# A weight shift done in place, two softmax norms on another engine, and a saturating add in the first block of tokens

## The chip, the cores and the metric

The kernel runs on one core of one Trainium2 chip. The core has five engines that run side by side: TensorE (PE; its weight loads are shown as PEld), VectorE (DVE), ScalarE (ACT), GpSimd (POOL) and SyncE (SP, which here only issues transfers). The metric is the device time of one execution in microseconds, lower is better.

## The reference

Three stages, each feeding the next. The attention is masked in two ways: the first half of the heads sees a window of 32 keys, the second half every fourth key of the last 128.

```
# attention: q, k, v are (4, 8, 576, 64)
scores = scale * q @ k.T
scores = where(mask, scores, -1e9); attn = softmax(scores)
x = (attn @ v) as (2304 tokens, 512)
# first feed-forward: w_in (512, 2048), w_out (2048, 512)
h = x @ w_in
x = (h * cos(h)) @ w_out
# second feed-forward: w1, w2, w3 (512, 768), w_out (768, 512)
h = maximum(maximum(x @ w1, x @ w2), x @ w3)
out = h @ w_out
```

The weights arrive as 64-bit floats, as the reference's setup draws them, and the kernel turns them into 32-bit floats on the chip.

## The kernel before, in words

**Precision.** A matrix product is made of three passes of a fast 32-bit format. Each operand is split into a high part and a low part (`g_hi` and `g_lo`, `w_hi` and `w_lo`), and the products high*high, low*high and high*low are summed in PSUM.

**Stages.** The tokens of the first feed-forward are cut into five blocks (four of 512, one of 256). First comes the attention of the 12 units that block 0 needs (about 7 to 48 us). Then `ff1` runs 16 steps per block, one per slice of 128 hidden columns. A step `s` makes `h` for its slice (12 matrix products, line 358), and the output sums for slice `s - 3` (12 products, line 401). `h` has two PSUM banks that alternate (`h_bank`, `bank_98` and `bank_99` in the rows; step 2 alone has `bank_97`), so step `s + 2` can start only when VectorE has read the bank of step `s` for the last time (line 390). In between stand the attention units of the next block: scores (lines 268 to 275), exponentials (217), norm (303 to 307), transposes (315), output (326 to 345).

**Steps 0 to 15 do one thing more.** They turn the 32 weight tiles of the first feed-forward from 64 into 32 bits: `w_exponent` on ScalarE (line 183) rescales the high words in place, `w_bits` on VectorE (lines 188 and 191) joins the words into `wx`, and `w_halves` splits the result on ScalarE (line 143, `w<-wx`) and GpSimd (line 208). `wx` has two buffers, and a buffer is free again when GpSimd is done with it. In block 1 and later, `raw_bits` (lines 437 and 440) does the same for the weights of the second feed-forward on tiles of half the size, and there the shift already writes in place.

**The cosine.** `ff1_reduce` brings the argument into the range of the sine table. The table `ENGINES` says which engine does what, with one entry for each of four phases: the attention of block 0, block 0 of `ff1` (16 steps), the blocks after that, and the last block. In phase 1 the entry `turns` is `"A"`: ScalarE makes the number of turns `kk` as a rounded integer (line 372), and VectorE makes `r = hv - 2 pi kk` (line 378) and clips it (line 381). Then ScalarE takes the sine (line 217), VectorE multiplies by `hv` (line 390) and the product is split (lines 143 and 392).

**Norms.** The entry `norm` of phase 0 is `"VPP"`: of the 12 units of the first attention, units 0, 3, 6 and 9 have their norm (line 307) on VectorE and the others on GpSimd.

**Order.** The code writes one program, and a scheduler with a cost model of its own sets the order of the instructions on each engine. So an edit in one place moves instructions around it too. Every engine runs its own instructions in that order, and one that waits holds up all that stand behind it.

Of the kernel before, what the change touches and what calls it, by code (L numbers as in the profile page):

```python
# [2 lines left out]

# [4 lines left out]

F32 = mybir.dt.float32
# [2 lines left out]
I32 = mybir.dt.int32  # L12
I64 = mybir.dt.int64
AF = mybir.ActivationFunctionType
ALU = mybir.AluOpType
# [34 lines left out]
ARG_HI = 1.5707960  # L50
ARG_LO = -4.7123880
# [5 lines left out]
ENGINES = {  # L57
    "w_hi": ("A", "A", "A", "V"),
    "w_lo": ("P", "P", "P", "PV"),
    "norm": ("VPP", "V", "V", "V"),  # L60
    "pt": ("A", "A", "V", "V"),
    "ring": ("A", "A", "V", "V"),
    "turns": ("V", "A", "V", "V"),
# [34 lines left out]
def body(  # L98
# [11 lines left out]
    nc = tc.nc  # L110
# [20 lines left out]
    def engine(work):  # L131
        names = ENGINES[work][phase[0]]
        turn[work] = turn.get(work, 0) + 1
        return names[(turn[work] - 1) % len(names)]
# [50 lines left out]
    def bits(x, w):  # L185
        pair = w.bitcast(I32).rearrange("p (n two) -> p n two", two=2)
        low, high = pair[:, :, 0], pair[:, :, 1]
        nc.vector.tensor_scalar(
            out=x, in0=high, scalar1=3, scalar2=None, op0=ALU.logical_shift_left
        )  # L190
        nc.vector.scalar_tensor_tensor(
            out=x, in0=low, scalar=29, in1=x, op0=ALU.logical_shift_right, op1=ALU.bitwise_or
        )

    def w_exponent(key):
# [2 lines left out]
    def w_bits(key):  # L198
        x = wx.tile([128, 512], I32, tag="x", name="wx")
        bits(x, words[key])  # L200
        words[key] = x.bitcast(F32)
# [13 lines left out]
    def activation(*args, **kw):  # L215
        with tc.issue_after(last_table[-1]) if last_table else nullcontext():
            last_table.append(nc.scalar.activation(*args, **kw).ins)  # L217
# [150 lines left out]
    def ff1_reduce(s, hv):  # L368

        kk = tmp.tile([128, TB], F32, tag="r", name="kk")[:, : hv.shape[-1]]  # L370
        if engine("turns") == "A":
            nc.scalar.activation(kk.bitcast(I32), hv, AF.Copy, scale=INV2PI, bias=0.25)
        else:
            nc.vector.tensor_scalar(  # L374
                out=kk.bitcast(I32), in0=hv, scalar1=INV2PI, scalar2=0.25, op0=ALU.mult, op1=ALU.add
            )
        r = tmp.tile([128, TB], F32, tag="r", name="r")[:, : hv.shape[-1]]
        nc.vector.scalar_tensor_tensor(  # L378
            out=r, in0=kk.bitcast(I32), scalar=-2.0 * math.pi, in1=hv, op0=ALU.mult, op1=ALU.add
        )  # L380
        nc.vector.tensor_scalar(  # L381
            out=r, in0=r, scalar1=ARG_HI, scalar2=ARG_LO, op0=ALU.min, op1=ALU.max
        )
        activation(r, r, AF.Sin, bias=hpi)
        g[s] = (hv, r)

# [447 lines left out]
    for s in range(NS + LAG):  # L834
# [17 lines left out]
        if s < NS:  # L852

            hv = (bank[3] if s == 2 else h_bank[(s + (s > 2)) % 2])[:, : BLOCKS[t]]
# [5 lines left out]
        for j, (kind, x, c) in enumerate(chunks):  # L860
            if kind == "h":
                hc(x, c)
                if x == NC - 1:
                    hvs[s] = hv
                    ff1_reduce(s, hv)
            else:
                t0, f0 = divmod(s - LAG, NF1)
                acc_chunk(STARTS[t0], f0 == 0, f0 == NF1 - 1, halves[("out", f0)], g[s - LAG], x)
            while done < len(pieces) and done * len(chunks) < (j + 1) * len(pieces):
                do, u = pieces[done]  # L870
                do(u)
                done += 1
            if j == 1:
                if s >= 1 and s - 1 < NS:
                    ff1_g(s - 1)
            if s < NF1:
                weights(STEP_WEIGHTS[s].count(j), WSLOTS)
            if j == 1:
                raw_exponent(s - NF1)
            if j == 5:  # L880
                raw_bits(s - NF1)
# [94 lines left out]
```

## Time and profile before

| what | value |
|---|---|
| median of 3 runs | 832.45 us (832.4 to 833.21) |
| the profiled execution | 830.6 us, its span 828.8 us |
| busy in the span: PE, DVE, ACT, POOL | 795.8, 571.3, 430.9, 134.1 us |
| mean granted TensorE clock | 0.983 of 2.4 GHz |

The span is the time from the first to the last instruction that the profiler saw on the core. What lies around it, 1.8 us here, is part of the time of the execution. A busy TensorE need not be one at its peak, since the ends of matrix products are modelled.

### The profile page before, as it was taken

What the parts mean: (1) busy time and instruction counts of PE and PEld (TensorE: products, weight loads), DVE (VectorE), ACT (ScalarE), POOL (GpSimd) and SP (SyncE); (2) the same over time, 40 slices, a digit from 0 to 9 for tenths busy, and PEclk for the clock granted to TensorE, in tenths of its full rate; (3) what the DMA queues carried; (4) which work ended last, traced back from release to release, by engine and by line L of the source; (5) the groups of instructions that cost most, each with busy time, mean ns of one, the idle gap of its engine ahead of it and who ended that gap; (6) DMA issues with size and microseconds to landing.
All of it is one profiled execution on the core that took longest, in us unless ns stands there. A gap on an engine that the chain in (4) does not pass through costs nothing.

```text
span 828.8 us, 12969 instructions
## 1 busy us (share of the span) xinstructions
PE 795.8 (96%) x4484; PEld 679.8 (82%) x4484; DVE 571.3 (69%) x1499; ACT 430.9 (52%) x1004; POOL 134.1 (16%) x120
## 2 busy tenths in 40 slices
PE   7867999999999999999999999999999999999998
PEld 6645767677777877777878889998899999999997
DVE  5888899768887788888686676878873355615540
ACT  5977988657765287774442234365452324422321
POOL 1354445410000000000000002225520000000000
PEclk8968999999999999999999999999999999999999
DMA  9982111234334343333020015636783778537812
GB/s 349 418 335 79 36 49 51 73 124 136 108 99 127 119 150 96 110 127 123 28 70 10 1 50 182 237 143 264 268 303 107 210 260 253 172 121 258 249 34 76
DMA packets 52625, 124.43 MB, mean 150 GB/s; under 512 B 5840, under 2 KB 18768, under 8 KB 52560
## 3 DMA queue, kind: packets, MB, share of 16 engines
q1 hardware_dynamic: 52560, 123.61, 43.8%
q8 instruction: 35, 0.57, 0.3%
q14 instruction: 30, 0.25, 0.1%
HBM read 91.34 MB, written 32.24 MB: 149 GB/s over the span
## 4 chain that ended last, share of the span: by engine, by line
PE 67%; DVE 12%; DMA 11%; ACT 4%; issue 3%; POOL 2%; SPq 1%; ACTq 0%; POOLq 0%; DVEq 0%
PE bank L586 20%; PE bank L401 16%; PE bank L358 15%; PE bank L651 9%; PE bank L268 3%; DMA w<-in_w_in 3%; DMA w<-in_w_out 2%; DMA wh<-in_w 2%; PE bank L326 2%; PE bank L315 1%; DVE ws L510 1%; DMA wd<-wh 1%; ACT e L217 1%; DMA raw<-wd 1%; DVE r L378 1%
## 5 line engine op out<-in xcount | busy, mean ns | idle before, releaser
L358 PE MATMUL bank<-ring,w 128*128 128x512 f32 (+1 forms) x960 | 235.3, 383 | 7.4 <-DVE r L390 6.3
L401 PE MATMUL bank<-gt,w 128*128 128x512 f32 (+1 forms) x960 | 225.3, 376 | 0.0
L586 PE MATMUL bank<-ring,wa 128*128 128x384 f32 x1134 | 200.5, 335 | 3.7 <-DVE mx L616 2.6
L586 PEld LDWEIGHTS bank<-ring,wa 128*128 128x128 f32 x1134 | 196.4, 188 | 6.2 <-DVE mx L616 3.7
L358 PEld LDWEIGHTS bank<-ring,w 128*128 128x128 f32 x960 | 166.4, 192 | 42.5 <-DVE r L390 8.2
L401 PEld LDWEIGHTS bank<-gt,w 128*128 128x128 f32 x960 | 164.9, 189 | 33.4 <-issue 0.3
L217 ACT ACTIVATE r<-r,hpi 128x512 f32<-128x512 f32 (+1 forms) x80 | 54.5, 681 | 93.9 <-DVE r L381 93.3
L217 ACT ACT_TABLE_LOAD x62 | 79.5, 1283 | 32.5 <-DVE r L381 25.6
L217 ACT ACTIVATE e<-e,m 96x128 f32<-96x128 f32 x192 | 74.8, 391 | 6.2 <-DVE m L275 5.6
L651 PE MATMUL bank<-g,w 128*128 128x384 f32 x432 | 76.3, 334 | 0.0
L651 PEld LDWEIGHTS bank<-g,w 128*128 128x128 f32 x432 | 75.0, 188 | 0.0
L390 DVE TENSOR_TENSOR r<-bank,r 128x512 f32<-128x512 f32 (+1 forms) x80 | 50.5, 632 | 21.5 <-ACT r L217 21.5
L139 POOL TENSOR_SCALAR gt<-r 128x512 fp32r<-128x512 f32 x24 | 16.1, 673 | 296.8 <-PE bank L401 229.2
L275 DVE CUSTOM_DVE_ANT_0 e<-bank,cs 96x128 f32<-96x128 f32 x192 | 45.7, 282 | 20.7 <-PE bank L271 10.1
L374 DVE TENSOR_SCALAR kk<-bank 128x512 int32<-128x512 f32 (+1 forms) x64 | 39.7, 621 | 19.2 <-PE bank L358 16.7
L208 POOL TENSOR_TENSOR w<-wx,w 128x512 fp32r<-128x512 f32 x32 | 44.7, 1410 | 48.8 <-ACT w L143 47.5
L378 DVE SCALAR_TENSOR_TENSOR r<-kk,bank 128x512 f32<-128x512 int32 (+1 forms) x80 | 50.3, 629 | 1.6 <-DMA x1d<-o 0.2
L392 DVE TENSOR_TENSOR gt<-r,gt 128x512 fp32r<-128x512 f32 (+1 forms) x65 | 40.4, 621 | 14.1 <-POOL gt L139 10.6
L268 PEld LDWEIGHTS bank<-qkv 64*96 64x96 f32 x288 | 26.0, 163 | 26.9 <-issue 8.7
L602 ACT COPY s<-bank 128x384 f32<-128x384 f32 x54 | 25.8, 478 | 37.9 <-PE bank L586 36.5
L268 PE MATMUL bank<-qkv 64*96 64x128 f32 x288 | 38.5, 295 | 6.9 <-DVE m L275 3.7
L620 DVE TENSOR_TENSOR s<-s,bank 128x384 f32<-128x384 f32 x36 | 19.8, 551 | 34.3 <-PE bank L586 34.2
(65 smaller groups left out, 848.7 us busy)
## 6 DMA issues: line engine op xcount, KB each, us to landing
wa<-opd SPq DMA_DIRECT2D x54, 512.0 KB, 4.6
opd<-wa SPq DMA_DIRECT2D x27, 512.0 KB, 2.8
qkv<-in_qkv SPq DMA_DIRECT2D x36, 336.0 KB, 2.9
wh<-in_w SPq DMA_DIRECT2D x36, 256.0 KB, 2.7
w<-in_w_in SPq DMA_DIRECT2D x16, 512.0 KB, 9.3
w<-in_w_out SPq DMA_DIRECT2D x16, 512.0 KB, 9.8
qkv<-in_qkv SPq DMA_DIRECT2D x12, 432.0 KB, 9.1
wd<-wh SPq DMA_DIRECT2D x36, 128.0 KB, 1.8
```

The source lines that it names most:

```text
L208: tensor("w_lo").tensor_tensor(out=w[:, 1, :], in0=x, in1=w[:, 0, :].bitcast(F32), op=ALU.subtract)
L217: last_table.append(nc.scalar.activation(*args, **kw).ins)
L268: nc.tensor.matmul(sv, q[rows], k[rows], start=True, stop=True)
L275: nc.vector.tensor_tensor_reduce(out=e[:, 2 * j + h, :], in0=places_of[j, h], in1=mask[:, kind, :], scale=-1.0 / math.sqrt(D), scalar=3e38 ...
L358: nc.tensor.matmul(hv, w[:, a, 128 * c : 128 * c + 128], ring[c][:, x, c0 : c0 + n_tok], start=n == 0 and j == 0, stop=n == NC - 1 and j == 2,
L374: nc.vector.tensor_scalar(out=kk.bitcast(I32), in0=hv, scalar1=INV2PI, scalar2=0.25, op0=ALU.mult, op1=ALU.add)
L378: nc.vector.scalar_tensor_tensor(out=r, in0=kk.bitcast(I32), scalar=-2.0 * math.pi, in1=hv, op0=ALU.mult, op1=ALU.add)
L390: nc.vector.tensor_tensor(out=r, in0=hv, in1=r, op=ALU.mult)
L392: tensor("g_lo").tensor_tensor(out=gt[:, 1, :], in0=r, in1=gt[:, 0, :].bitcast(F32), op=ALU.subtract)
L401: nc.tensor.matmul(a_dm, w[:, a, 128 * dm : 128 * dm + 128], gt[:, x, :], start=first and n == 0, stop=last and n == 2,)
L586: nc.tensor.matmul(out, ops[q][a][:, x, 128 * c : 128 * c + 128], b_op(b, c)[:, y], start=first and c == 0 and n == 0, stop=c == 1 and n == 2,
L651: nc.tensor.matmul(a, wo[2 * f + r][:, x, 128 * dm : 128 * dm + 128], g2[f, r, n][:, y], start=f == 0 and r == 0 and k == 0, stop=f == NF2 ...
```

## The change

Three edits. In `w_bits` the shift of the high words (line 188) writes into the tile of the 64-bit weights itself and not into `wx`; the joining instruction (line 191) reads both words there and is the first to write `wx`. In `ENGINES` the norm's entry for phase 0 names all 12 units one by one: units 10 and 11 go from GpSimd to VectorE, the others stay. In `ff1_reduce`, where `turns` is `"A"` (block 0 alone), ScalarE also multiplies `kk` by `-2 pi`, and one VectorE instruction, `TENSOR_ADD_SAT`, adds `hv` and clips; the two VectorE instructions of lines 378 and 381 stay for the other blocks.

```
-    "norm": ("VPP", "V", "V", "V"),
+    "norm": ("VPPVPPVPPVVV", "V", "V", "V"),
...
         nc.vector.tensor_scalar(
-            out=x, in0=high, scalar1=3, scalar2=None, op0=ALU.logical_shift_left
+            out=high, in0=high, scalar1=3, scalar2=None, op0=ALU.logical_shift_left
         )
         nc.vector.scalar_tensor_tensor(
-            out=x, in0=low, scalar=29, in1=x, op0=ALU.logical_shift_right, op1=ALU.bitwise_or
+            out=x, in0=low, scalar=29, in1=high, op0=ALU.logical_shift_right, op1=ALU.bitwise_or
         )
...
-        if engine("turns") == "A":
+        e = engine("turns")
+        if e == "A":
             nc.scalar.activation(kk.bitcast(I32), hv, AF.Copy, scale=INV2PI, bias=0.25)
...
-        nc.vector.scalar_tensor_tensor(
-            out=r, in0=kk.bitcast(I32), scalar=-2.0 * math.pi, in1=hv, op0=ALU.mult, op1=ALU.add
-        )
-        nc.vector.tensor_scalar(
-            out=r, in0=r, scalar1=ARG_HI, scalar2=ARG_LO, op0=ALU.min, op1=ALU.max
-        )
+        if e == "A":
+
+            nc.scalar.activation(r, kk.bitcast(I32), AF.Copy, scale=-2.0 * math.pi)
+            nc.vector._custom_dve(dve_ops.TENSOR_ADD_SAT, out=r, in0=hv, in1=r, s0=ARG_HI, s1=ARG_LO)
+        else:
+            nc.vector.scalar_tensor_tensor(
+                out=r, in0=kk.bitcast(I32), scalar=-2.0 * math.pi, in1=hv, op0=ALU.mult, op1=ALU.add
+            )
+            nc.vector.tensor_scalar(
+                out=r, in0=r, scalar1=ARG_HI, scalar2=ARG_LO, op0=ALU.min, op1=ALU.max
+            )
```

What the scheduler makes of it, at two places. The first is ScalarE from the first `kk` of block 0 (bank_98 holds step 0, bank_99 step 1, bank_97 step 2) to the first sines. Before:

```order
L372 ACTIVATE kk<-bank_98 128x512
L143 CAST w<-wx 128x512
L372 ACTIVATE kk<-bank_99 128x512
L183 ACTIVATE w_284<-w_284 128x512
L143 CAST w<-wx 128x512
L217 ACT_TABLE_LOAD
L217 ACTIVATE r<-r,hpi 128x512 x2
L183 ACTIVATE w_286<-w_286 128x512
L372 ACTIVATE kk<-bank_97 128x512
```

The same stretch of the changed kernel, where line 373 is the old 372 and line 381 is the new multiplication:

```order
L373 ACTIVATE kk<-bank_98 128x512
L143 CAST w<-wx 128x512
L381 ACTIVATE r<-kk 128x512
L373 ACTIVATE kk<-bank_99 128x512
L143 CAST w<-wx 128x512
L217 ACT_TABLE_LOAD
L217 ACTIVATE r<-r,hpi 128x512
L381 ACTIVATE r<-kk 128x512
L183 ACTIVATE w_286<-w_286 128x512
L373 ACTIVATE kk<-bank_97 128x512
L217 ACTIVATE r<-r,hpi 128x512
```

The multiplication stands one weight cast behind its `kk`, and the second sine has moved behind the second multiplication, one exponent instruction and the third `kk`.

The second place is VectorE from the first high part of a product (`gt<-r`, step 0) to the first scores of block 1 (line 275). Before:

```order
L143 CAST gt<-r 128x512
L378 SCALAR_TENSOR_TENSOR r<-kk,bank_97 128x512
L188 TENSOR_SCALAR wx<-w_286 128x512
L381 TENSOR_SCALAR r<-r 128x512
L191 SCALAR_TENSOR_TENSOR wx<-w_286,wx 128x512
L188 TENSOR_SCALAR wx<-w_288 128x512
L191 SCALAR_TENSOR_TENSOR wx<-w_288,wx 128x512
L188 TENSOR_SCALAR wx<-w_290 128x512
L275 ISA e,m<-bank_100,cs 96x128
```

The same stretch of the changed kernel, where line 382 is the saturating add and line 396 the old 390:

```order
L143 CAST gt<-r 128x512
L188 TENSOR_SCALAR w_286<-w_286 128x512
L191 SCALAR_TENSOR_TENSOR wx<-w_286 128x512
L396 TENSOR_TENSOR r<-bank_99,r 128x512
L382 ISA r<-bank_97,r 128x512
L188 TENSOR_SCALAR w_288<-w_288 128x512
L191 SCALAR_TENSOR_TENSOR wx<-w_288 128x512
L275 ISA e,m<-bank_100,cs 96x128
```

One shift and one instruction of the reduction have gone from in front of the scores, and the last product of step 1 (bank_99), which stood ahead of the cast before, has come in.

## Rows read from the trace of the kernel before

**Rows 1.** The page's first part: busy time, share of the span, instructions.

```profile
PE 795.8 (96%) x4484; PEld 679.8 (82%) x4484; DVE 571.3 (69%) x1499; ACT 430.9 (52%) x1004; POOL 134.1 (16%) x120
```

**Rows 2.** Windows by stage: window, PE, PEld, DVE, ACT, POOL busy, granted clock, DMA.

```profile
48.00:70.00 22.00, 13.87 (x48) 10.05 (x48) 19.69 (x34) 16.43 (x31) 12.26 (x9) 0.72 0.76 287
70.00:160.00 90.00, 85.95 (x477) 63.01 (x476) 77.34 (x208) 75.13 (x192) 40.61 (x29) 0.98 0.15 45
400.00:500.00 100.00, 100.00 (x479) 82.07 (x478) 69.18 (x138) 34.35 (x64) 6.34 (x9) 1.00 0.11 35
```

**Rows 3.** Timeline, end of the first attention: start, duration, instruction, idle before.

```profile
41.48 1.37 POOL L307 TENSOR_TENSOR e<-e,z 96x512 f32<-96x512 f32 x1 [0.71 <-DVE z L304]
41.91 0.96 DVE L303 TENSOR_SCALAR z<-z 96x4 f32<-96x4 f32 x1
42.90 0.65 PE L315 MATMUL bank<-cs,e 96*128 96x96 f32 x4 [1.31 <-POOL e L307]
...
44.34 0.74 PE L315 MATMUL bank<-cs,e 96*128 96x96 f32 x3 [0.79 <-POOL e L307]
45.55 1.48 DVE L188 TENSOR_SCALAR wx<-w 128x512 int32<-128x512 int32 x1 [2.23 <-POOL w L208]
```

**Rows 4.** Timeline, from the first `kk` to step 3 on TensorE.

```profile
52.32 0.60 ACT L372 ACTIVATE kk<-bank 128x512 int32<-128x512 f32 x1 [1.95 <-PE bank L358]
...
53.50 1.30 POOL L208 TENSOR_TENSOR w<-wx,w 128x512 fp32r<-128x512 f32 x1 [2.03 <-ACT w L143]
53.55 1.79 DVE L191 SCALAR_TENSOR_TENSOR wx<-w,wx 128x512 int32<-128x512 int32 x1
...
56.07 1.28 ACT L217 ACT_TABLE_LOAD   x1
...
57.37 1.40 ACT L217 ACTIVATE r<-r,hpi 128x512 f32<-128x512 f32 x2
...
58.53 1.27 DVE L390 TENSOR_TENSOR r<-bank,r 128x512 f32<-128x512 f32 x2
...
59.27 4.21 PE L358 MATMUL bank<-ring,w 128*128 128x512 f32 x9 [4.31 <-DVE r L390]
```

**Rows 5.** Timeline, in front of the first scores of block 1.

```profile
61.72 1.51 DVE L381 TENSOR_SCALAR r<-r 128x512 f32<-128x512 f32 x1
...
63.15 1.75 DVE L191 SCALAR_TENSOR_TENSOR wx<-w,wx 128x512 int32<-128x512 int32 x1
...
67.13 1.47 DVE L188 TENSOR_SCALAR wx<-w 128x512 int32<-128x512 int32 x1 [1.17 <-POOL w L208]
...
69.29 0.88 PE L268 MATMUL bank<-qkv 64*96 64x128 f32 x8 [3.75 <-DVE m L275]
```

**Rows 6.** Groups on DVE, 70 to 160 us: busy, mean ns, idle before.

```profile
L275 DVE CUSTOM_DVE_ANT_0 e<-bank,cs 96x128 f32<-96x128 f32 x44 | 10.6, 279 | 4.4 <-PE bank L268 2.7 <-PE bank L315 1.3 <-ACT kk L372 0.3
...
L378 DVE SCALAR_TENSOR_TENSOR r<-kk,bank 128x512 f32<-128x512 int32 x11 | 7.4, 674 | 0.0
L381 DVE TENSOR_SCALAR r<-r 128x512 f32<-128x512 f32 x11 | 6.4, 586 | 0.0
```

**Rows 7.** Groups on ACT, 70 to 160 us.

```profile
L143 ACT CAST w<-wx 128x512 fp32r<-128x512 f32 x19 | 11.5, 616 | 3.4 <-DVE wx L191 3.4
L183 ACT ACTIVATE w<-w 128x512 f32<-128x512 f32 x15 | 9.7, 676 | 0.0
```

**Rows 8.** Chain that ended last, share by line, 70 to 160 us.

```profile
by line: PE bank L401 15.8%; PE bank L358 13.9%; issue 13.8%; PE bank L268 7.0%; POOL w L208 7.0%; ACT e L217 4.9%; DVE e L307 4.8%; DVE wx L188 4.0%; DVE wx L191 4.0%; DVE r L381 3.4%; DVE e L275 3.2%; PE bank L326 2.8%; DVE ring L345 2.6%
```

**Rows 9.** Lines by themselves: least, median and most ns; first and last start.

```profile
L188 DVE TENSOR_SCALAR wx<-w x32: 393/417/1502, 11.5 to 155.3; 128x512 int32<-128x512 int32 x32
L191 DVE SCALAR_TENSOR_TENSOR wx<-w,wx x32: 673/688/1793, 12.8 to 156.3; 128x512 int32<-128x512 int32 x32
L437 DVE TENSOR_SCALAR wh<-wh x48: 258/285/299, 161.5 to 398.1; 128x256 int32<-128x256 int32 x48
L378 DVE SCALAR_TENSOR_TENSOR r<-kk,bank x80: 410/679/689, 52.9 to 543.2; 128x512 f32<-128x512 int32 x64, 128x256 f32<-128x256 int32 x16
```

More of the change, by code (lines that the diff above doesn't have):

```diff
@@ L5 @@
 import concourse.tile as tile
-from concourse import mybir
+from concourse import dve_ops, mybir
 from concourse._compat import with_exitstack
```

## The prediction

> **What bounds the kernel now.** I read the busy times of the page first: TensorE is busy for 96% of the span, so a gain has to come from where it is not, or from where it is slow [rows 1]. The windows by stage say where that is. Late in the kernel it has no idle time (400 to 500 us: 100.00 of 100). From 48 to 70 us it is busy for 13.87 of 22 us at a granted clock of 0.72, and from 70 to 160 us for 85.95 of 90 while VectorE has 77.34 and ScalarE 75.13 [rows 2]. That is block 0 of `ff1`, the only place where `w_bits` and the changed branch of the cosine run.
>
> Then I read the timeline at TensorE's two long waits there. They add up to 4.31 + 3.75 = 8.06 of the 8.13 idle us between 48 and 70 [rows 2, 4, 5]. The first ends when VectorE has made the product of step 0 (line 390), the second when it has read the first scores of block 1 (line 275). What the reader is to see in the rows ahead of them are VectorE instructions that last far too long. The join of line 191 takes 0.688 us in the median, but 1.79 where it starts 0.05 us after a GpSimd split; it ends at 55.34, the split at 54.80, so it did nearly all its work after the split [rows 4, 9]. The shift of line 188 (median 0.417, most 1.502), line 381 (1.51) and even the tiny line 303 (0.96 us for 4 columns, until GpSimd's norm ended) behave alike [rows 3, 5, 9]. Line 378, with one input in PSUM, is never held: most 0.689 against a median of 0.679 [rows 9]. So VectorE is the engine that is late here, and part of its lateness is being held behind GpSimd.
>
> **The shift in place.** Same instruction, other destination. Line 437 is that form on half the size: 0.285 us for 256 elements, where line 188 takes 0.417 for 512 [rows 9]. The difference, 0.132 us for 256 elements, is 0.52 ns each; line 191's 0.688 for 512 is at least twice that. So the form in place runs at the fast rate too: one that didn't would take more than 0.285 for 256. So the price is 0, and the shift can still be held by GpSimd. What goes is its wait for a free `wx`, 2.23 and 1.17 us in two places [rows 3, 5]. It doesn't vanish: the join of line 191 is now the one that waits for the buffer. Only the shift's own 0.417 moves in front of the wait. I count 0.4 us, once, on the path; bounds 0 and 2.2 (the first wait wholly gone).
>
> **The two norms.** Unit 10's norm ran on GpSimd from 41.48 for 1.37 us, and TensorE went on at 42.90; unit 11's let it go on at 44.34, after 1.31 and 0.79 us of idling [rows 3]. On VectorE a norm reads 512 elements from two SBUF inputs, as line 191 does: 0.688 us if not held [rows 9]. It would be ready near 42.6, 0.3 earlier. But GpSimd is then free to take the next weight split, and this holds VectorE at unit 11's norm for up to 1.3 us [rows 4]: 43.5 at best, 44.6 at worst. I take 0, bounds -0.3 and +0.9.
>
> **The cosine, first wait.** From the start of the first `kk` (52.32) to TensorE's next product (59.27) it is 6.95 us now [rows 4]. In the new order ScalarE runs `kk`, a weight cast, the multiplication, the second `kk`, another cast, the table load and the first sine. Durations: 0.60 for `kk`; 0.616 for a cast; the multiplication is new, and its nearest rows are two ScalarE instructions over 512 elements in SBUF, 0.616 and 0.676, so 0.65 [rows 4, 7]; 1.28 for the table; half of 1.40 for a sine and half of 1.27 for the product [rows 4]. Sum: 0.60 + 0.62 + 0.65 + 0.60 + 0.62 + 1.28 + 0.70 + 0.64 = 5.71. The saturating add lies under the second `kk`, the cast and the table load, with 2.50 us of cover; without it it would cost its 0.69. Gain 6.95 - 5.71 = 1.2. Each of the two casts waits for a join, and a held join is 1.1 late [rows 4]: bounds -1.0 and, if ScalarE's instructions overlap, +2.0.
>
> The add itself is not in this trace. A custom VectorE instruction of 128 elements takes 0.279 us, a plain one of 512 with the same kind of inputs 0.674 [rows 6]. With 0.674 as the lower bound and four times 0.279, 1.12, as the upper, I take 0.685: the small custom instruction shows no extra start cost. One input in PSUM, like line 378, so I expect it never to be held.
>
> **The cosine, second wait.** From the cast in `gt` to the scores VectorE now has, unheld, 0.68 + 3 x 0.417 + 0.42 + 2 x 0.688 = 3.73 us of work (lines 378, 188, 381, 191), and rows 5 show 1.09 + 1.06 + 1.05 us of holding and 1.17 of waiting on top, 4.37 together. The new order has 2 x 0.417 + 2 x 0.688 + 0.68 + 0.685 = 3.58 of work, and four instructions there can be held at some 1.1 each. None held gives all of TensorE's 3.75; all four nothing. With two held: 4.37 - 2.2 + 0.15 = 2.3. Behind the scores stand the exponentials and with them all attention of block 1, so this is not given back at once.
>
> **The cosine, steps after 70 us.** VectorE loses 11 x (0.674 + 0.586) and gets 11 x 0.685: 6.3 us less of 77.34. ScalarE gets 11 x 0.65 = 7.2 more on 75.13, so 82.3 us of work [rows 2, 6]. Not all of the relief counts. The chain of waits has line 381 on it for 3.4% of these 90 us, 3.1 us [rows 8]; that is my term. Bounds: 0, and 90 - 82.3 = 7.7, where ScalarE would never idle.
>
> **Sum.** 0 + 0.4 + 1.2 + 2.3 + 3.1 = 7.0 us. The profiled execution took 830.6 (span 828.8 and 1.8 around it), so 823.6 for its like; the median of before is 1.85 above it: 825.4. All upper bounds together (0.9 + 2.2 + 2.0 + 3.75 + 7.7) would be 816, all lower ones (-0.3 - 1.0) 833.8. About 0.2%, 1.7 us, is what a measurement tells from no change.
>
> **Rivals.** *ScalarE fills up.* With 82.3 us of work in a stretch that is to shrink to 87, an engine that runs in order and also carries exponentials and table loads has little slack. Then the term of 3.1 goes and one held cast takes 1.1 from the first wait: 832.45 - 2.8 = 829.6. For it: its busy share would be 95%. Against: VectorE was at 86% and still on the path, so the load alone does not decide.
>
> *Slower: the sine comes later in every step.* From `kk` to sine it is 0.60 + 0.674 + 0.586 = 1.86 us now, and 0.60 + 0.62 + 0.65 + 0.69 = 2.56 with one cast in between, 0.7 later; 1.8 later where that cast waits for a held join. The place is the cast between lines 373 and 381 in the changed order. Over the 11 steps this is 7.7 to 20 us if the two `h` banks make TensorE wait for it each time. It decides from about ten steps at 0.7 or four at 1.8, which cancels the 7.0. Halfway, at 1.05 a step, it gives 11.6 - 7.0 = 4.6 slower: 837. Against: TensorE idles only 4.05 us in the 90 [rows 2], so the banks leave room. The Trainium skill (ScalarE: Activation LUTs, Rules for kernel authors) advises VectorE and not ScalarE for `mul` and `add`, and by that rule the move is a loss; the rows agree that the multiplication was free on VectorE, inside line 378, and show that VectorE is the late one.
>
> *Hidden anyway.* The holding by GpSimd finds another VectorE instruction each time, and the two waits stay: 832.
>
> *More.* Less idling may also keep the granted clock up (0.72 in this stretch [rows 2]), and most of the 7.7 comes in: 818.
>
> **How the numbers follow.** Forecast (821 to 829) 0.55; ScalarE fills up 0.13; slower 0.11; hidden 0.10; more 0.11. Faster 0.79, same 0.10, slower 0.11. The range 818 to 832.5 leaves out the slower case and about half of the largest.
>
> **What would show it.** The add at 0.67 to 0.70 us, none above 0.75; the multiplication at 0.62 to 0.68; line 188 still at 0.417 in the median, with no wait for `wx`, and waits in front of line 191 instead; TensorE's two waits near 3.1 and 1.5 us; VectorE's share of the stretch down by some 6 us, ScalarE's up by 7. Wrong if the add is held behind GpSimd, if the sines wait for the multiplication, or if the time after block 0 moves by itself.

## The result, and the profile after

The changed kernel takes 827.0 us in the median of 5 runs (823.42 to 828.71), beside 833.21 (832.4 to 835.62) for the kernel before on the same chip. The ratio is 0.9911, with a 95% interval of 0.9894 to 0.9927: faster by 0.9%, some 7.4 us. All ratios below are of 4 to 12 runs of a kernel against the kernel before, timed beside it, with the 95% interval in brackets; gains in us go by the ratio. The profiled execution took 827.17 us, its span 825.4. In the changed kernel line 372 has become 373, 390 is 396, 401 is 407 and 411 is 417; line 381 is the new multiplication and 382 the saturating add.

The page's first part, and the windows by stage (columns as in [rows 2]):

```profile
PE 793.4 (96%) x4484; PEld 678.6 (82%) x4484; DVE 567.1 (69%) x1485; ACT 439.2 (53%) x1020; POOL 132.9 (16%) x118
```

```profile
48.00:70.00 22.00, 17.16 (x70) 11.79 (x68) 17.81 (x47) 19.05 (x43) 13.12 (x9) 0.77 0.74 287
70.00:160.00 90.00, 87.52 (x489) 64.80 (x489) 73.98 (x179) 79.64 (x197) 41.71 (x30) 1.00 0.16 44
```

Against [rows 2], TensorE is busy 3.3 us more in the 22 us of the ramp and 1.6 us more in the 90 behind it. VectorE has lost 3.4 us there and ScalarE has gained 4.5.

The timeline of the changed kernel: the last norms, then from the first `kk` to step 3, then in front of the scores.

```profile
42.98 0.55 PE L315 MATMUL bank<-cs,e 96*128 96x96 f32 x4 [0.96 <-DVE e L307]
43.10 1.30 POOL L208 TENSOR_TENSOR w<-wx,w 128x512 fp32r<-128x512 f32 x1 [1.92 <-ACT w L143]
...
43.51 1.43 DVE L307 TENSOR_TENSOR e<-e,z 96x512 f32<-96x512 f32 x1
...
45.09 0.39 PE L315 MATMUL bank<-cs,e 96*128 96x96 f32 x1 [1.56 <-DVE e L307]
...
51.95 0.60 ACT L373 ACTIVATE kk<-bank 128x512 int32<-128x512 f32 x1 [1.42 <-PE bank L358]
...
52.96 0.63 ACT L381 ACTIVATE r<-kk 128x512 f32<-128x512 int32 x1
...
53.62 0.69 DVE L382 CUSTOM_DVE_ANT_0 r<-bank,r 128x512 f32<-128x512 f32 x1 [0.65 <-ACT r L381]
...
54.60 1.28 ACT L217 ACT_TABLE_LOAD   x1
...
55.90 0.72 ACT L217 ACTIVATE r<-r,hpi 128x512 f32<-128x512 f32 x1
...
56.65 0.69 DVE L396 TENSOR_TENSOR r<-bank,r 128x512 f32<-128x512 f32 x1 [1.49 <-ACT r L217]
...
57.40 2.62 PE L358 MATMUL bank<-ring,w 128*128 128x512 f32 x7 [3.17 <-DVE r L396]
...
58.71 1.58 DVE L191 SCALAR_TENSOR_TENSOR wx<-w 128x512 int32<-128x512 int32 x1
...
61.93 1.59 DVE L191 SCALAR_TENSOR_TENSOR wx<-w 128x512 int32<-128x512 int32 x1
...
64.21 0.89 PE L268 MATMUL bank<-qkv 64*96 64x128 f32 x8 [1.67 <-DVE m L275]
```

The add ends at 54.31, under the second `kk`, a cast and the table load, so it is hidden as worked out. TensorE's waits are 3.17 and 1.67 us, where [rows 4, 5] have 4.31 and 3.75. In front of the scores two joins are held.

The lines by themselves (least, median, most ns), answering to [rows 9]:

```profile
L188 DVE TENSOR_SCALAR w<-w x32: 396/418/1492, 11.6 to 155.0; 128x512 int32<-128x512 int32 x32
...
L191 DVE SCALAR_TENSOR_TENSOR wx<-w x32: 675/693/1728, 12.9 to 155.6; 128x512 int32<-128x512 int32 x32
...
L381 ACT ACTIVATE r<-kk x16: 612/634/654, 53.0 to 165.0; 128x512 f32<-128x512 int32 x16
...
L382 DVE CUSTOM_DVE_ANT_0 r<-bank,r x16: 673/680/693, 53.6 to 165.7; 128x512 f32<-128x512 f32 x16
...
L417 DVE COPY o<-bank x10: 425/685/693, 184.1 to 544.8; 128x512 f32<-128x512 f32 x8, 128x256 f32<-128x256 f32 x2
```

The add takes 0.680 us and at most 0.693: never held. The shift in place has kept its 0.418. The last row marks the end of block 0, by the first copy of its sums: 184.1 us. In the kernel before that copy reads:

```profile
L411 DVE COPY o<-bank x10: 423/683/692, 190.0 to 548.4; 128x512 f32<-128x512 f32 x8, 128x256 f32<-128x256 f32 x2
```

So the profiled execution is 5.9 us ahead when block 0 ends. This splits into 0.4 before the first `kk` (52.32 to 51.95), 1.5 from there to step 3 (6.95 to 5.45), 3.2 from step 3 to the scores (10.02 to 6.81) and 0.8 from the scores to that copy (120.71 to 119.89). The third part is not all gain: three products that stood ahead of the scores now stand behind them, and their 1.1 us (6.27 to 5.14 of work between the two waits) have moved to the last part. So the shares are 0.4, 1.5, 2.1 and 1.9.

### The profile page after: what moved, and what is told of

Read it like the earlier page. It is cut to its first block, busy times and chain, and to the rows that moved or that the text cites. A ratio compares the mean times of both kernels' runs of the same rounds, so it can differ in the third digit from the quotient of the medians.

```text
span 825.4 us, 12970 instructions
## 1 busy us (share of the span) xinstructions
PE 793.4 (96%) x4484; PEld 678.6 (82%) x4484; DVE 567.1 (69%) x1485; ACT 439.2 (53%) x1020; POOL 132.9 (16%) x118
## 4 chain that ended last, share of the span: by engine, by line
PE 70%; DVE 13%; DMA 7%; ACT 5%; issue 3%; POOL 2%; SPq 0%; ACTq 0%; DVEq 0%; POOLq 0%
PE bank L592 19%; PE bank L407 17%; PE bank L358 16%; PE bank L657 9%; PE bank L268 4%; PE bank L326 2%; DMA raw<-wd 2%; DMA wh<-in_w 2%; PE bank L315 2%; DVE ws L516 1%; DMA wd<-wh 1%; DVE r L396 1%; ACT e L217 1%; ACT r L217 1%; DVE r L384 1%
## 5 line engine op out<-in xcount | busy, mean ns | idle before, releaser
L358 PE MATMUL bank<-ring,w 128*128 128x512 f32 (+1 forms) x960 | 232.3, 381 | 6.2 <-DVE r L396 5.5
L183 ACT ACTIVATE wh<-wh 128x256 f32<-128x256 f32 x48 | 20.7, 435 | 41.2 <-DMA wh<-in_w 29.2
```

The lines of the kernel that those rows point to most:

```text
L358: nc.tensor.matmul(hv, w[:, a, 128 * c : 128 * c + 128], ring[c][:, x, c0 : c0 + n_tok], start=n == 0 and j == 0, stop=n == NC - 1 and j == 2,
```

## The experiments

The theory (T): VectorE is the late engine in block 0 because GpSimd holds it, and what counts of the change is that the cosine now asks less of VectorE, in a form that is not held. The rivals: that the waits for `wx` or the two norms did it (W); that one instruction that can't be held, the add, is enough, wherever the multiplication is made (H); that ScalarE has slack for whatever it is given (S).

**The split of the cosine alone.** The third edit alone, on the kernel before.

```
-        nc.vector.scalar_tensor_tensor(
-            out=r, in0=kk.bitcast(I32), scalar=-2.0 * math.pi, in1=hv, op0=ALU.mult, op1=ALU.add
-        )
...
+            nc.scalar.activation(r, kk.bitcast(I32), AF.Copy, scale=-2.0 * math.pi)
+            nc.vector._custom_dve(dve_ops.TENSOR_ADD_SAT, out=r, in0=hv, in1=r, s0=ARG_HI, s1=ARG_LO)
```

> Only the cosine's split (ScalarE multiplies, VectorE adds and clips in one instruction) is kept; the shift writes to its own buffer and the norms are divided as before. Theory A (the add carries the gain, by one VectorE instruction fewer in each step of block 0 and by one that GpSimd cannot hold): 0.992 of the kernel before, 826 to 828 us, TensorE's wait for the product of step 0 near 3.2 us as with all three edits. Theory B (the three edits work only together, since holding by GpSimd just finds another instruction): 0.996 to 1.000, 829 to 833 us.

Measured: 828.55 us, 0.9949 [0.9928, 0.9969]. It carries 4.2 of the 7.4 us by itself, which lies between the two ranges and decides for neither theory. TensorE's wait for the product of step 0 is 2.98 us, as expected. But from step 3 to the scores of block 1 it takes 9.18 us, where it took 10.02 before and takes 6.81 with the whole change:

```profile
58.12 2.35 PE L358 MATMUL bank<-ring,w 128*128 128x512 f32 x9 [2.98 <-DVE r L396]
...
67.30 1.37 PE L268 MATMUL bank<-qkv 64*96 64x128 f32 x8 [4.87 <-DVE m L275]
```

**The shift in place alone.**

```
-            out=x, in0=high, scalar1=3, scalar2=None, op0=ALU.logical_shift_left
+            out=high, in0=high, scalar1=3, scalar2=None, op0=ALU.logical_shift_left
...
-            out=x, in0=low, scalar=29, in1=x, op0=ALU.logical_shift_right, op1=ALU.bitwise_or
+            out=x, in0=low, scalar=29, in1=high, op0=ALU.logical_shift_right, op1=ALU.bitwise_or
```

> Only the shift in place is kept. Theory A: within 0.1% of the kernel before, at most 0.9 us faster; the shift no longer waits for its buffer, the join behind it is held longer by about as much (mean of line 191 above 1.0 us from 40 to 170 us, where it was 0.835). Theory C (the wait for the buffer was the stall that mattered): 0.996 or less, 830 us or less.

Measured: 831.64 us, 0.9972 [0.9958, 0.9986], 2.3 us: more than the 0.9 that theory A allows, less than theory C asks for. From 40 to 170 us no shift waits for its buffer, and the joins are held longer, but to 0.899 us in the mean and not above 1.0.

**The norms alone.**

```
-    "norm": ("VPP", "V", "V", "V"),
+    "norm": ("VPPVPPVPPVVV", "V", "V", "V"),
```

> Only the norms of units 10 and 11 move to VectorE. Theory A: between 0.3 us slower and 0.9 us faster, so 0.999 to 1.000: unit 10's transposes come 0.3 us earlier and unit 11's norm is held by GpSimd's weight split. Rival (GpSimd free earlier for the splits, so the whole ramp comes earlier): 0.997, 830.5 us.

Measured: 832.11 us, 0.9986 [0.9972, 0.9999], 1.2 us, hardly told from nothing. The interval holds theory A's 0.999; the rival's 0.997 is just outside it.

**Both of these without the split.** From the changed kernel, lines 378 and 381 are put back:

```
-            nc.scalar.activation(r, kk.bitcast(I32), AF.Copy, scale=-2.0 * math.pi)
-            nc.vector._custom_dve(dve_ops.TENSOR_ADD_SAT, out=r, in0=hv, in1=r, s0=ARG_HI, s1=ARG_LO)
...
+        nc.vector.tensor_scalar(
+            out=r, in0=r, scalar1=ARG_HI, scalar2=ARG_LO, op0=ALU.min, op1=ALU.max
+        )
```

> The shift in place and the norms together, without the cosine's split. Theory A: 0.999 to 1.000, 832 to 833.5 us. Theory B (the edits need one another): 0.995 to 0.997, about half of the whole change's gain.

Measured: 835.06 us, 1.0024 [1.001, 1.0038]. Each of the two edits gains a little alone, and together they lose 2 us, more than either theory had; to the whole change it is 9.4. The edits don't add up. Two windows of this run show one thing that goes wrong:

```profile
36.00:110.00 74.00, 61.56 (x307) 44.18 (x306) 61.13 (x168) 56.95 (x144) 31.08 (x22) 0.82 0.42 159
68.00:82.00 14.00, 13.52 (x42) 9.38 (x42) 6.94 (x34) 6.70 (x22) 0.91 (x1) 0.51 0.01 1
```

Its timeline has TensorE's two long waits right ahead of the second window:

```profile
58.90 3.35 PE L358 MATMUL bank<-ring,w 128*128 128x512 f32 x7 [5.21 <-DVE r L390]
...
68.48 1.37 PE L268 MATMUL bank<-qkv 64*96 64x128 f32 x8 [3.37 <-DVE m L275]
```

From 68 to 82 us TensorE idles for 0.48 of 14 us and runs at a granted clock of 0.51, about the lower level of 1.2 GHz: 42 products fill 13.52 us, where in the kernel before 66 fill 12.07 us of the same window at 0.88. Over 36 to 110 us the clock is 0.82 here, 0.86 before and 0.91 after the change (before, then after):

```profile
36.00:110.00 74.00, 60.06 (x326) 42.89 (x325) 62.55 (x172) 59.76 (x150) 33.47 (x25) 0.86 0.43 161
```

```profile
36.00:110.00 74.00, 63.51 (x353) 45.78 (x352) 62.09 (x172) 64.53 (x160) 35.95 (x26) 0.91 0.44 166
```

That the low clock costs here is shown; that it is all of the loss against the kernel before is not, since this run's profiled execution (832.33 us) is 2.7 under its own median.

**The change without the norms, and without the shift in place.** Two kernels; each puts back one edit as shown above.

> The cosine's split and the shift in place, with the norms divided as before. Theory A (the cosine's split is worth nearly all): 0.991 to 0.993 of the kernel before, the same as the whole change within 0.1%. If the norms carry a part of their own: 0.994 or more.

> The cosine's split and the norms, with the shift writing to its own buffer. Theory A: 0.991 to 0.993. If the shift in place carries a part of its own (VectorE waited 5.3 us for the buffer before): 0.995 or more.

Measured: 827.01 us, 0.9941 [0.9924, 0.9959] without the norms; 827.68 us, 0.9933 [0.9917, 0.9949] without the shift in place. These are 4.9 and 5.6 us, so beside the split's 4.2 either edit adds 0.7 to 1.3 us, within the intervals, and both together add 3.2, which the intervals only just part (0.9927 and 0.9928). Both ratios lie just above theory A's range, so that the split is worth nearly all is not shown. W falls as the main cause, since the two edits gain nothing without the split; but some of the gain comes only with them. One place shows it. From step 3 to the scores it takes 9.18 us with the split alone, 9.19 with the shift in place beside it, 10.06 with the norms alone, but with the split and the norms 6.86, as in the whole change:

```profile
58.87 2.68 PE L358 MATMUL bank<-ring,w 128*128 128x512 f32 x7 [3.21 <-DVE r L396]
...
65.73 0.88 PE L268 MATMUL bank<-qkv 64*96 64x128 f32 x8 [1.73 <-DVE m L275]
```

**The multiplication on VectorE.** The whole change, but VectorE multiplies, with its input in SBUF; the add stays.

```
-            nc.scalar.activation(r, kk.bitcast(I32), AF.Copy, scale=-2.0 * math.pi)
+            nc.vector.tensor_scalar(
+                out=r, in0=kk.bitcast(I32), scalar1=-2.0 * math.pi, scalar2=None, op0=ALU.mult
+            )
```

> The whole change, but the multiplication by -2 pi runs on VectorE (one input in SBUF, 0.42 us when not held) and the saturating add stays. Theory A (the gain comes from taking work off VectorE): most of it goes, 0.998 to 1.001, 831.5 to 834 us, since VectorE has two instructions per step again, 0.42 and 0.68, and GpSimd can hold the first. Rival (the gain comes from the last instruction before the sine being one that GpSimd cannot hold): 0.993 to 0.995.

Measured: 838.84 us, 1.007 [1.0055, 1.0084], slower than before. The groups on VectorE from 70 to 160 us (columns as in [rows 6]; line 384 is the add):

```profile
L381 DVE TENSOR_SCALAR r<-kk 128x512 f32<-128x512 int32 x10 | 9.2, 925 | 0.0
...
L384 DVE CUSTOM_DVE_ANT_0 r<-bank,r 128x512 f32<-128x512 f32 x10 | 6.8, 678 | 0.0
```

The add is not held here either, but the multiplication is (0.925 us in the mean, its least 0.411), and the end of block 0 comes at 196.2 us. VectorE has as many of these instructions as in the kernel without the split (1.0024), and the time is above that one's, and above theory A's range, too: the two take 0.925 + 0.678 = 1.60 us a step, where lines 378 and 381 took 0.674 + 0.586 = 1.26 [rows 6]. H falls: the add does not help while the multiplication beside it can be held; taking the work off VectorE does.

**The multiplication twice.** ScalarE does it two times, with the same result, on the way to the sine.

```
             nc.scalar.activation(r, kk.bitcast(I32), AF.Copy, scale=-2.0 * math.pi)
+            nc.scalar.activation(r, kk.bitcast(I32), AF.Copy, scale=-2.0 * math.pi)
```

> The whole change with ScalarE's multiplication done twice in each step of block 0 (same result), so 16 more instructions of 0.63 us on ScalarE and 0.63 us more between kk and the sine. If ScalarE still has slack in block 0: at most 2 us above the whole change, 0.992 to 0.9945. If ScalarE has become the engine that bounds block 0 (79.64 us of work in the 90 from 70 to 160 us): up to 16 x 0.54 = 8.6 us above, 0.999 to 1.002.

Measured: 831.84 us, 0.9987 [0.9971, 1.0004]. 16 instructions of 0.632 us, 10.1 us on ScalarE, take 6.3 of the 7.4 us away. The runs fall apart by the clock: three with a mean granted clock of 0.990 took 827.49 to 829.87 us, nine at 0.978 to 0.984 took 830.86 to 834.24, and the profile is of the slowest. In it TensorE waited 2.42 us for line 345 until 122.64 us, and from 122 to 128 us the clock was 0.66; in the changed kernel it was 1.00 from 120 to 130 us. So a part of this loss goes with the clock. TensorE waits from 40 to 180 us (sum, times, longest) for the product of line 396, here 397:

```profile
PE bank L358 <- DVE r L397: 6.4, 3, 4.2
```

**The same load off the way to the sine.** An extra instruction in which ScalarE overwrites `kk` after its last use; nothing reads it.

```
+        if e == "A":
+            nc.scalar.activation(kk, kk.bitcast(I32), AF.Copy, scale=-2.0 * math.pi)
```

> The whole change with one extra ScalarE instruction of 0.63 us in each of the 16 steps, which reads kk after the multiplication and whose result nobody reads. In the order it stands between the multiplication and the sine, where the saturating add runs on VectorE, so it adds work to ScalarE but not to the way from kk to the sine. If the run with the multiplication done twice lost its 6 us to ScalarE's load: about as much here, 0.997 to 1.000 of the kernel before. If it lost them to the longer way to the sine: 0.991 to 0.9935.

Measured: 829.27 us, 0.9965 [0.9948, 0.9981], 4.5 us slower than the change for 10.1 us of work (16 x 0.630). Who waits is in the same view, first this run, then the changed kernel:

```profile
PE bank L358 <- DVE r L398: 4.0, 4, 3.2
PE bank L326 <- ACT pt L143: 3.0, 3, 2.2
```

```profile
PE bank L358 <- DVE r L396: 3.2, 1, 3.2
...
PE bank L315 <- DVE m L275: 1.2, 1, 1.2
PE bank L326 <- ACT pt L143: 0.8, 2, 0.6
```

TensorE now waits 3.0 and not 0.8 us for ScalarE's copies of the transposed attention (line 143). It also waits 4.0 and not 3.2 us for the product behind the sine, so the added instruction is not wholly off that way. S falls: load alone on ScalarE costs, though the ratio is just under the range expected for it. By the middles most of what the double multiplication lost is load (4.5 of 6.3 us); that the rest is its place in front of the sine is not shown, since the two intervals overlap.

**The high part of the product on VectorE alone.** The whole change, and the casts `gt<-r` of block 0, of which ScalarE makes every third, all go to VectorE, to relieve ScalarE.

```
-    "g_hi": ("P", "VAV", "AP", "A"),
+    "g_hi": ("P", "V", "AP", "A"),
```

> The whole change, and in block 0 the high parts of the products (line 143, gt from r) all on VectorE, where ScalarE made every third: 5 instructions of 0.62 us fewer on ScalarE, 5 of 0.42 us or more on VectorE. If ScalarE's load now bounds block 0: 1 to 3 us faster than the whole change, 0.988 to 0.990. If VectorE still does: 0.992 to 0.994.

Measured: 832.69 us, 1.0012 [0.9997, 1.0028]: a miss, the whole gain is gone. The cast needs a free `gt` buffer, and VectorE, which runs in order, stands and waits for it. Its wait from 40 to 180 us, and what TensorE then waits for:

```profile
DVE gt L143 <- PE bank L407: 9.1, 9, 2.4
```

```profile
PE bank L315 <- DVE m L275: 5.0, 4, 1.9
```

In the changed kernel the first is 4.1 us and the second 1.2. That this wait makes all of the loss is argued, not shown.

**The low part of the weights on VectorE.** 27 of GpSimd's 32 weight splits (line 208) move to VectorE: first on top of the change, then on the kernel before with none of the three edits.

```
-    "w_lo": ("P", "P", "P", "PV"),
+    "w_lo": ("P", "V", "P", "PV"),
```

> The whole change, and in block 0 of ff1 the weights' low parts (line 208) on VectorE: 26 or so instructions of 0.69 us more there, and GpSimd left with the products' low parts alone. If the long shifts and joins come from GpSimd's work: line 191's mean from 70 to 160 us falls from about 1.1 to under 0.8 us and line 188's under 0.5, and the time lies within 3 us of the whole change although VectorE has 18 us more of its own work. If they are long for another reason: the means stay, and the time is 8 us or more above.

> The kernel before with one edit: in block 0 of ff1 the weights' low parts (line 208) on VectorE and not on GpSimd. None of the change's three edits. VectorE gets 26 or so instructions of 0.69 us more, and GpSimd can hold it much less. If being held is a main reason why VectorE is late: 0.990 to 0.996 of the kernel before, about as good as the change itself, with line 381's mean from 70 to 160 us falling from 0.586 to 0.45 or less. If the number of VectorE's instructions is what counts: 1.000 to 1.010, since it has 14 us more work from 70 to 160 us on top of 77.

Measured: 821.66 us, 0.9867 [0.9844, 0.9891] on top; 821.61 us, 0.9858 [0.9835, 0.9881] alone. Both beat both kernels, and with this one word changed the three edits are worth nothing that can be measured. On top of the change, the mean of line 191 from 70 to 160 us falls from 1.108 to 0.742 us and that of line 188 from 0.573 to 0.495, as expected. For the second, the windows, VectorE's groups from 70 to 160 us, and TensorE's two waits:

```profile
48.00:70.00 22.00, 17.38 (x81) 12.45 (x80) 19.21 (x57) 19.65 (x42) 4.31 (x2) 0.88 0.75 287
70.00:160.00 90.00, 89.52 (x500) 66.45 (x499) 83.82 (x225) 74.98 (x186) 19.97 (x12) 1.00 0.19 55
```

```profile
L191 DVE SCALAR_TENSOR_TENSOR wx<-w,wx 128x512 int32<-128x512 int32 x19 | 16.2, 853 | 0.1
L208 DVE TENSOR_TENSOR w<-wx,w 128x512 fp32r<-128x512 f32 x21 | 15.7, 752 | 0.0
L188 DVE TENSOR_SCALAR wx<-w 128x512 int32<-128x512 int32 x19 | 9.6, 515 | 0.0
...
L381 DVE TENSOR_SCALAR r<-r 128x512 f32<-128x512 f32 x13 | 5.4, 418 | 0.0
```

```profile
56.11 4.14 PE L358 MATMUL bank<-ring,w 128*128 128x512 f32 x10 [3.22 <-DVE r L390]
...
63.41 0.89 PE L268 MATMUL bank<-qkv 64*96 64x128 f32 x8 [1.40 <-DVE m L275]
```

VectorE gets 21 instructions and 15.7 us more, and is busy only 6.5 us longer (83.82 against 77.34), though it does more of its other work in the window. Line 381, 0.586 us in the mean of [rows 6], is back at 0.418: it is hardly held any more. The shifts are held less (0.515 us for 0.742 before), the joins rather more (0.853 for 0.782); GpSimd still makes the products' low parts (line 392). TensorE is busy for 89.52 of 90 us, and block 0 ends at 177.2 us. T's expectation is met, and the gain goes further than I had taken it: the engine with the most work in the stretch finished earlier with more of it. What this run does not part is the holding from what else changed: a split takes 0.68 us on VectorE and 1.30 on GpSimd, so a `wx` comes free sooner, and the clock from 48 to 70 us is 0.88, not 0.72. So the holding as the cause of the whole 11.8 us is argued, not shown.

## Why the prediction was right, and where its terms were off

825.4 us was predicted and 827.0 measured, inside the range; by the ratio the gain is 7.4 us and by the prediction 7.0. Term by term, with the shares of the profiled pair:

- *Norms, 0, and the shift's 0.4.* TensorE went on at 42.98 and not at 42.6, but this execution was 0.3 us behind there (unit 10's line 304 starts at 41.45 us, and at 41.14 before); the wait fell from 1.31 to 0.96, about as foreseen. The second norm was held at 43.51 for 1.43 us behind a weight split, as foreseen; its wait grew from 0.79 to 1.56 us. At the first `kk` the kernel is 0.4 us ahead, as much as the two terms' sum, but that is luck: TensorE began the 18 products ahead of it 0.33 us later and made them faster, at a granted clock of 0.75 and not 0.61 from 48 to 55 us. Before, then after, the window and the 18 products:

```profile
48.00:55.00 7.00, 6.88 (x18) 5.12 (x18) 5.89 (x9) 4.53 (x9) 4.23 (x3) 0.61 0.88 293
...
48.07 6.88 PE L358 MATMUL bank<-ring,w 128*128 128x512 f32 x18 [0.33 <-DVE ring L345]
```

```profile
48.00:55.00 7.00, 6.22 (x24) 4.54 (x22) 5.82 (x9) 5.56 (x12) 4.47 (x4) 0.75 0.78 274
...
48.40 5.82 PE L358 MATMUL bank<-ring,w 128*128 128x512 f32 x18
```

- *The shift in place.* No shift waits for `wx` any more, but the wait did not move to the join as I had said; the holding did. Over 40 to 170 us the groups before and after are:

```profile
L191 DVE SCALAR_TENSOR_TENSOR wx<-w,wx 128x512 int32<-128x512 int32 x27 | 22.4, 835 | 0.3
L188 DVE TENSOR_SCALAR wx<-w 128x512 int32<-128x512 int32 x27 | 21.8, 817 | 5.3 <-POOL w L208 5.3
```

```profile
L191 DVE SCALAR_TENSOR_TENSOR wx<-w 128x512 int32<-128x512 int32 x27 | 29.6, 1098 | 1.6
L188 DVE TENSOR_SCALAR w<-w 128x512 int32<-128x512 int32 x27 | 16.0, 597 | 0.7 <-ACT w L183 0.7
```

  With the idle time it is 49.8 us before and 47.9 after: 5.3 us of waiting went, the shift lost 5.8 and the join gained 7.2. Alone, this edit (2.3 us) and the norms (1.2) each came out just above their upper bounds of 2.2 and 0.9, which their intervals hold.
- *First wait, 1.2.* From `kk` to step 3 it took 5.45 us where 5.71 was worked out: 1.5. The multiplication took 0.634 for 0.65, the add 0.680 for 0.685. This term is the best borne out: the stretch takes 5.45 to 5.48 us in the four profiles with the split (alone, with either of the other edits, with both), and 5.76 (the norms alone, with no join held there) to 7.50 us in the four without it.
- *Second wait, 2.3.* It fell from 3.75 to 1.67, 2.1, with two of the instructions in front of it held, as assumed. But its sum had left out that the first of the three shifts was held too (at 60.66 us, 1.14 us long); with that it would have been 3.0. And the term stood under the cosine alone, while the profiles show it only where the norms have moved too: from step 3 to the scores the split by itself gains 0.8 us, the norms by themselves nothing, both 3.2, with the same three products behind the scores as in the whole change. What in the new order does it stays open. So the size came out, but not by the working given.
- *Steps after 70 us, 3.1.* This is the term that was mis-sized in the profile: 1.9. TensorE's idle time in the 90 us went from 4.05 to 2.48. VectorE's relief was 3.4 and not 6 us, since the joins were held longer, and the double load on ScalarE, which I had taken as free below its idle time, has a price: 4.5 us for 10.1 of work. The multiplication is another 16 x 0.634 = 10.1 us; at that rate, an estimate, it gives back about as much.

These make 5.9 at the end of block 0, for 7.0. At the end of the spans 3.4 us are left, so the time after block 0 moved by itself, which the prediction had named as a sign of being wrong. Between the first copy of block 0's sums and the last product of line 358 it took 351.4 us before, 353.7 after, and between 351.1 and 354.3 in all the profiles of this study; the double multiplication, whose block 0 ended as late as before's, took 354.3 too. So part of the 2.5 us is scatter between executions; whether the rest was truly given back stays open. The timed runs don't show it: they give 6.2 us between the medians and 7.4 by the ratio.

Of the rivals, *hidden anyway* falls by the two waits. *The sine comes later* falls in this kernel: from 40 to 180 us TensorE waits only once for line 396, the 3.17 us shown, so the two `h` banks bore the rest; with the sine 0.63 us later still, in the double multiplication, there are three such waits and 6.4 us, so that is where it begins to cost. (Halfway between that rival's 0.7 and 1.8 us a step is 1.25, not 1.05, which would have made it about 839 us, not 837.) The Trainium skill (ScalarE: Activation LUTs, Rules for kernel authors) would have the multiplication on VectorE; here that is 838.84 against 827.0 us, and the measurement decides. *ScalarE fills up* did not decide the sign but is part of the answer: ScalarE did 79.64 us in the 90, not 82.3, and has little free slack. *More*, by the clock, is half there: over 36 to 110 us the granted clock is 0.91 for 0.86, yet the time did not come near 818.

## What to carry to other kernels

When an instruction's longest time is two or three times its median, look at what ran beside it before counting how long its engine is busy: moving the disturber's work onto the disturbed engine (27 splits here, 11.8 us gained) was worth more than shortening that engine's own work (7.4 us), though that run does not part the holding from the faster split. An engine that is busy 88% of a stretch (ScalarE, 79.64 of 90 us) and runs in order has little slack to give away: 10 us more on ScalarE cost 4.5 us although nothing waited for the added result. Undo edits one at a time and also in pairs, since two edits that gained 2.3 and 1.2 us alone lost 2.0 together.

## What the runs showed of the hardware that was not expected

A `tensor_scalar` on VectorE that reads SBUF was held behind GpSimd also as a multiplication of integers (0.411 to 1.511 us in the run with the multiplication on VectorE), while a custom add of 512 elements with one input in PSUM was not held in any of its 16 executions (0.673 to 0.693) and cost the same as the plain two-input instruction it replaced (0.679). The Trainium skill (SBUF — State Buffer, Who interferes with whom) states that a VectorE instruction with at most one SBUF input, outside its two-port modes, does not contend with GpSimd, and that one in such a mode does; these rows fit that, though none shows an instruction's mode, and add the size: up to 1.1 us for each instruction held.
